# Quarter products of a pair issued in one piece, channel 128 moved ahead, 64-row transfers in a Fourier and MLP kernel

## The chip, the cores and the metric

One core of a Trainium2 chip runs the whole program. The metric is device time in microseconds (us), and lower is better. A measurement of this kernel can tell differences of about 0.2% (1.6 us).

## The reference

Float32 data, 2 batches of 3136 x 256 (sequence x channels), three blocks one after the other:

```python
# block 1: Fourier mixing along the sequence
X = np.fft.rfft(x, axis=1)
Yr, Yi = complex product of X with w_r + i w_i, plus bias
Y = soft threshold of Yr and Yi by 0.01
a = np.fft.irfft(Y, n=3136, axis=1)
# block 2: layer norm and MLP, 256 -> 1024 -> 256
m = a + relu(layernorm(a) * g_ln @ w_ch1) @ w_ch2
# block 3: 2-D Fourier transform, then a second MLP
u = m + real(np.fft.fft(np.fft.fft(m, axis=1), axis=2))
out = u + relu(layernorm(u) @ w1) @ w2
```

## The kernel before

3136 is 49 x 64, so each transform along the sequence is split into one of length 49 and one of length 64. Block 2 runs in 13 chunks (`mlp1`) and block 3 in 13 chunks (`mlp2`), mostly of 512 rows. A chunk has a first layer (`l1`, eight steps of six matmuls into a `psa` bank, L217 to L219; then relu on ScalarE, L744, and the rest term on VectorE, L746) and a second layer (`l2`, one step for each 128 rows: pairs of matmuls L763 and L764 into a `psb` bank, then VectorE adds L769 and L770). The input of a chunk is transposed through memory: VectorE transposes blocks (L684), `dT<-q` stores 512 KB (L690), `q<-dT` loads it back (L698), and then ScalarE and VectorE form the two operands of `l1` from `q`, as `u0r<-q` (L199 and L207).

The change concerns **stage 4**, the class `Stage98`: the transform of length 49 over block 2's output `dX` (one scratch tensor in DRAM of 98 x 8192 for each batch), giving `dA`. For each of eight column groups `g` a `step` does this:

- `load` (L380): two DMAs of 49 rows x 1024 columns into partitions 0 to 48 and 64 to 112 of a slot. One of four slots is used for each group; groups are loaded up to three ahead.
- `fold` (L392 to L394, GpSimd): sums and differences of mirrored channels, for batch 1 only. Batch 0 does the same after the product instead (`fold_last`, ScalarE L445 and VectorE L449 and L450).
- `quad` (L403): four quarter products of 49 x 64 by 49 x 512, over `e` (output half) and `s` (input half), into two `psc` banks. There are three `psc` banks.
- copies of both banks to `o` (ScalarE, L199), and two columns of channel 128, `o<-mid` (ScalarE for batch 0, GpSimd L453 for batch 1).
- four stores `dA<-o` of 49 x 512 (L455).

Channel 128 has no mirror partner. `middle` loads it for all groups (L412, `m<-dX`), and `middle2`, called from the step of `g == 0`, makes its product with a quad of 16 columns and copies it to `mid`.

Batch 0's stage 4 runs inside chunks 8 to 10 of `mlp1` and batch 1's inside chunks 1 to 3 of `mlp2`. Two tables say at which step (chunk, layer, step) each `g` is emitted; the later pieces of block 3 (`r<-dA`, L815; products L831 and L856 into `psc`; sums with `yb`, L861 to L868) read `dA`.

```python
STAGE4_AT = ((8, "l1", 7), (8, "l2", 1), (8, "l2", 3), (9, "l1", 1), (9, "l1", 6), (9, "l2", 2), (10, "l1", 3), (10, "l2", 0))
STAGE4_MLP2 = ((1, "l1", 3), (1, "l2", 0), (1, "l2", 2), (2, "l1", 1), (2, "l1", 5), (2, "l2", 1), (3, "l1", 1), (3, "l1", 5))
```

The order on each engine is set by a scheduler that simulates the program; `tc.issue_after(ins)` forces what is written under it to come behind `ins`, and `mark[...]` keeps the last instruction of a kind for that use. Each engine then runs its instructions strictly in that order. Nearly all DMAs are issued by SP, in one queue order, and each of them also waits for the DMA that stands eight places before it in that order, since eight completion semaphores are used in turn. The final rows of `mlp2` load `yb<-dX` (L635) and store `out_dram<-o` (L779), some of them with an outer size of 2 or with one row for each of 128 partitions.

Of the kernel before, what the change touches and what calls it, by code (L numbers as in the profile page):

```python
# [36 lines left out]
SOON = {"b": (3, 5), "mix": (5, 7), "stats": (("l1", 6), ("l2", 0)), "norm": (("l2", 0),) * 4, "flip": (("l2", 1), ("l2", 2))}  # L37
LATE = {"b": (4, 6), "mix": (6, 7), "stats": (("l1", 7), ("l2", 0)), "norm": (("l2", 0),) * 4, "flip": (("l2", 2), ("l2", 3))}
LAND_AT = ("l1", 3)
TRANS1_AT = (4, 6)  # L40
PREP0_AT = (23, 24, 26, 28)
L2_BEHIND = 7
APPLY_POOL = ()
STAGE4_AT = ((8, "l1", 7), (8, "l2", 1), (8, "l2", 3), (9, "l1", 1), (9, "l1", 6), (9, "l2", 2), (10, "l1", 3), (10, "l2", 0))
STAGE4_MLP2 = ((1, "l1", 3), (1, "l2", 0), (1, "l2", 2), (2, "l1", 1), (2, "l1", 5), (2, "l2", 1), (3, "l1", 1), (3, "l1", 5))
STAGE4_FROM = ((7, "l2", 0), (0, "l1", 5))
WARM_UP = 10
TB = 2
# [111 lines left out]
def fourier_moe_kernel(ctx, tc, x, w_r, w_i, b_r, b_i, g_ln, w11, w12, w21, w22,  # L160
# [59 lines left out]
        mark["pe"] = getattr(ins, "ins", ins)  # L220


    def scratch(nm):
        return [dp.tile([NQ, FW], F32, name=f"{nm}{b}") for b in range(NB)]

    dY, dX1, dA2 = (scratch(n) for n in ("dY", "dX1", "dA2"))

    def by_k1(t, k1, n):

# [1 line left out]
        return v[(k1 - 1) * 32768:(k1 - 1 + n) * 32768].rearrange("(k p c) -> p k c", k=n, c=D)  # L231

    def k1_zero(t):
        return t.rearrange("q f -> (q f)")[NK * 32768:].rearrange("(p c) -> p c", c=D)

    def rows(t, r0, n, nt):
        v = t.rearrange("q (j c) -> (q j) c", c=D)
# [24 lines left out]
    def behind(f):  # L262

        with ExitStack() as es:
            for k, ins in mark.items():
                if k not in ("pe", "clip", "hi"):
                    es.enter_context(tc.issue_after(ins))
            f()

# [94 lines left out]
    class Stage98:  # L364
# [1 line left out]


        def __init__(self, src, dst, tag):
            self.src, self.dst = (a.rearrange("(n s) f -> s n f", s=2) for a in (src, dst))
            self.tag, self.raw, self.out = tag, {}, {}  # L370
            self.fold_last = src is dX1[0]
            self.g = self.nl = self.ns = 0

        def load(self):
            g = self.nl
            if g >= 8:
                return
            t = next(s98_ring)
            for s in range(2):
                sp.dma_start(out=t[64 * s:64 * s + N1], in_=self.src[s][:, g * 1024:(g + 1) * 1024])  # L380
            self.raw[g] = [t[:, e * 512:(e + 1) * 512] for e in range(2)]
            self.nl += 1

# [14 lines left out]
        def quad(self, c, v, n=512):  # L398

            ps = [psum(self.tag) for _ in range(2)]  # L400
            for e in range(2):
                for s in range(2):
                    ins = nc.tensor.matmul(out=ps[s][64 * e:64 * e + 64, 0:n], lhsT=ca[64 * s:64 * s + N1, c:c + 64],  # L403
                                           rhs=v[e][64 * s:64 * s + N1], start=True, stop=True)
            mark["pe"] = getattr(ins, "ins", ins)
            return ps

        def middle(self):

            t = wk.tile([128, 32], F32, tag="m98", name="m98", bufs=1)  # L410
            for s in range(2):
                sp.dma_start(out=t[64 * s:64 * s + N1], in_=self.src[s].rearrange("n (j c) -> n j c", c=D)[:, :, 128])  # L412
            self.mid_in = t.rearrange("q (g e j) -> q e g j", e=2, j=2)

        def middle2(self):
# [14 lines left out]
        def step(self):  # L430
            g = self.g
            if g >= 8:
                return
            if g == 0:
                self.middle2()
            if self.nl <= g + 3:
                self.load()
            self.fold()
            ps = self.quad(0, self.raw.pop(g))
            for s in range(2):  # L440
                o = wk.tile([128, 512], F32, tag="r98", name="o98", bufs=R98) if self.fold_last and s else next(o98_ring)
                mid = self.mid[:, s, 2 * g:2 * g + 2]
                if self.fold_last:
                    v, w = (a.rearrange("q (j c) -> q j c", c=D) for a in (ps[s], o))
                    ins = nc.scalar.activation(out=w[:, :, 0:128], in_=v[:, :, 0:128], func=AF.Copy)  # L445
                    with tc.issue_after(getattr(ins, "ins", ins)):
                        a_copy(w[:, :, 128], mid)
                    lo, hi = w[:, :, 1:128], v[:, :, 255:128:-1]
                    nc.vector.tensor_tensor(out=w[:, :, 129:256], in0=lo, in1=hi, op=ALU.subtract)  # L449
                    nc.vector.tensor_tensor(out=lo, in0=lo, in1=hi, op=ALU.add)  # L450
                else:
                    a_copy(o, ps[s])
                    nc.gpsimd.tensor_copy(o[:, 128:512:256], mid)  # L453
                for e in range(2):
                    sp.dma_start(out=self.dst[s][:, (2 * g + e) * 512:(2 * g + e + 1) * 512], in_=o[64 * e:64 * e + N1])  # L455
            self.g += 1


# [156 lines left out]
    class Chunk:  # L615
# [112 lines left out]
        def l1(self, f):  # L728
            n = self.nt * 128
            (w1h, w1l), _ = self.wv  # L730
            ps = psum("a")
            fs = slice(f * 128, (f + 1) * 128)
            with ExitStack() as es:
                if self is mlp1[0] and f:
                    es.enter_context(tc.issue_after(self.pe))
                for c in range(2):
                    mm3r(ps[:, 0:n], w1h[:, c, fs], w1l[:, c, fs], self.xh[:, c, 0:n], self.xl[:, c, 0:n],
                         c == 0, c == 1)
            if f == L2_BEHIND:
# [12 lines left out]

        def l2(self, i):
            _, w2 = self.wv
            if not self.stored:
                self.o = oslot()
            self.stored += 1
            ps = psum("b")
            ts_ = slice(i * 128, (i + 1) * 128)
            with tc.issue_after(self.pe if self is mlp2[-1] and self.stored > 1 else self.last):  # L760
                for f in range(NF):
                    h, l = self.h[f]
                    nc.tensor.matmul(out=ps, lhsT=h[:, ts_], rhs=w2[:, f, :], start=f == 0, stop=False)  # L763
                    ins = nc.tensor.matmul(out=ps[:, 0:D], lhsT=l[:, ts_], rhs=w2[:, f, 0:D], start=False,  # L764
                                           stop=f == NF - 1)
            self.pe = getattr(ins, "ins", ins)

            o = self.o[:, i, :]
            nc.vector.tensor_tensor(out=o, in0=ps[:, 0:D], in1=self.y[:, i, :], op=ALU.add)  # L769
            nc.vector.tensor_tensor(out=o, in0=ps[:, D:2 * D], in1=o, op=ALU.add)  # L770
# [99 lines left out]
    def chunks2(plan, wv):  # L870
        cs = []
        for pairs in plan:
            lo, st, nt = [], [], 0
            for pr in pairs:
                for src, lst in ((dX1, lo), (out, st)):
                    for h, (b, k1) in enumerate(pr):
                        v = src[b] if src is out else src[b].rearrange("q (j c) -> (q j) c", c=D)
# [92 lines left out]
        todo.setdefault(k, []).append(f)  # L970
    for k, f in zip(MLP1_AT, mlp1_w[1:]):
        todo.setdefault(k, []).append(f)
    mlp1 = chunks1(0, wv1) + chunks1(1, wv1)
    mlp1[0].flipped = mlp1[1].flipped = False

# [217 lines left out]
    hook(2, "l2", 2, store3(4, range(4, 7)))  # L1193
    hook(*STAGE4_FROM[0], s4[0].start)
    hook(8, "l1", 1, after(8, 1, s4[0].ahead))
    for k, part, i in STAGE4_AT:
        hook(k, part, i, in_turn(mlp1, k, s4[0].step))
    mlp1[2].load()
# [47 lines left out]
```

## Time and profile before

| | us |
|---|---|
| median of 3 runs | 795.63 (795.11 to 795.73) |
| the profiled execution, whole time | 795.9 |
| its span, first to last instruction | 794.1 |
| TensorE (PE) busy | 782.5 (99%) |
| VectorE (DVE) busy | 550.6 (69%) |
| ScalarE (ACT) busy | 365.0 (46%) |
| GpSimd (POOL) busy | 127.5 (16%) |

The stretch of stage 4 is 354 to 420 us for batch 0 and 500 to 580 us for batch 1. A wait row names who waited, for whom, the us in total, the number of times and the longest. In a row of instructions, `[1.77 <-DVE mv L644]` is idle time before it and what ended it, and the us column is the length of one instruction, which for pipelined matmuls is longer than their spacing; the spacing is read from the start times. The granted clock of TensorE has two levels here, full and half; a window's figure is the mean (0.83 means that it was at half for a part).

### The profile page before, as it was taken

To read this page: it belongs to the slowest core of one execution; us is meant where nothing else is said; L and a number is where in the kernel's file an instruction comes from. 1 tells how busy PE (TensorE), PEld (TensorE's weight loads), DVE (VectorE), ACT (ScalarE), POOL (GpSimd) and SP (SyncE) were. 2 spreads that over 40 slices of the span, in tenths; PEclk is the share of its full clock that TensorE was granted. 3 is DMA by queue.
4 is the path that set the end of the run, shared out by engine and by line. 5 is a ranking of instruction groups with operands and counts; after the bars stand their busy time and mean duration, and the time that the engine had idled before them with its cause. 6 is when DMAs were issued, how large, how long until landed. Compare 5 with 4: busy or idle time off the path is not lost.

```text
span 794.1 us, 12190 instructions
## 1 busy us (share of the span) xinstructions
PE 782.5 (99%) x4348; PEld 652.9 (82%) x4348; DVE 550.6 (69%) x1253; ACT 365.0 (46%) x792; POOL 127.5 (16%) x146
## 2 busy tenths in 40 slices
PE   9999999999999999999999999998999999999997
PEld 3989977978888889976777988766788898888886
DVE  6799978687856988766666776456555757656643
ACT  0543356447954444645542344345443535444421
POOL 0465322254510111100000001243100000000000
PEclk9999999999999999999999999999999999999999
DMA  8950200621266323464543336534443334422211
GB/s 216 273 162 35 80 1 1 216 110 39 68 212 225 109 100 112 150 183 163 187 127 123 100 100 182 154 116 137 132 138 96 112 123 120 109 70 74 62 34 40
DMA packets 78047, 95.07 MB, mean 120 GB/s; under 512 B 17428, under 2 KB 59194, under 8 KB 77792
## 3 DMA queue, kind: packets, MB, share of 16 engines
q1 hardware_dynamic: 77908, 94.24, 38.3%
q8 instruction: 34, 0.56, 0.3%
q14 instruction: 25, 0.20, 0.1%
q10 hardware_dynamic: 80, 0.07, 0.0%
HBM read 56.80 MB, written 37.49 MB: 119 GB/s over the span
## 4 chain that ended last, share of the span: by engine, by line
PE 80%; DMA 9%; DVE 6%; issue 2%; SPq 1%; ACT 1%; POOL 1%; POOLq 0%; DVEq 0%; ACTq 0%
PE psb L763 21%; PE psa L217 11%; PE psb L764 11%; PE psa L219 10%; PE psa L218 10%; PE psb L511 5%; PE psc L831 2%; DMA q<-dT 2%; DMA dA<-o 2%; PE psc L356 2%; PE psa L478 2%; PE psc L403 2%; DMA q<-in_x_dram 1%; PE psc L856 1%; PE psc L532 1%
## 5 line engine op out<-in xcount | busy, mean ns | idle before, releaser
L744 ACT ACTIVATE h<-psa 128x512 fp32r<-128x512 f32 (+2 forms) x208 | 117.5, 572 | 209.2 <-PE psa L219 153.7
L746 DVE SCALAR_TENSOR_TENSOR h<-psa,h 128x512 fp32r<-128x512 f32 (+2 forms) x208 | 134.9, 653 | 63.5 <-ACT h L744 59.8
L763 PE MATMUL psb<-r2b,h 128*128 128x512 f32 x392 | 138.5, 400 | 1.8 <-DVE mv L644 1.8
L763 PE MATMUL psb<-r3a,h 128*128 128x512 f32 x392 | 137.3, 396 | 0.0
L764 PE MATMUL psb<-r2b,h 128*128 128x256 f32 x392 | 106.9, 282 | 0.0
L764 PE MATMUL psb<-r3a,h 128*128 128x256 f32 x392 | 106.1, 281 | 0.0
L511 PE MATMUL psb<-wm,h 128*128 128x256 f32 (+1 forms) x600 | 90.4, 296 | 0.2 <-DVE w L517 0.2
L763 PEld LDWEIGHTS psb<-r2b,h 128*128 128x128 f32 x392 | 72.5, 189 | 19.0 <-issue 3.8
L763 PEld LDWEIGHTS psb<-r3a,h 128*128 128x128 f32 x392 | 71.8, 188 | 16.3 <-ACT h L744 0.8
L511 PEld LDWEIGHTS psb<-wm,h 128*128 128x128 f32 (+1 forms) x600 | 78.1, 188 | 7.7 <-issue 5.6
L217 PE MATMUL psa<-u0r,r2b 128*128 128x512 f32 (+2 forms) x208 | 82.4, 396 | 2.0 <-ACT u0r L199 1.5
L217 PE MATMUL psa<-u0r,r3a 128*128 128x512 f32 (+1 forms) x208 | 80.0, 384 | 0.1
L219 PE MATMUL psa<-u0r,r2b 128*128 128x512 f32 (+2 forms) x208 | 79.5, 386 | 0.0
L218 PE MATMUL psa<-u0r,r2b 128*128 128x512 f32 (+2 forms) x208 | 79.2, 381 | 0.0
L218 PE MATMUL psa<-u0r,r3a 128*128 128x512 f32 (+1 forms) x208 | 78.8, 379 | 0.0
L764 PEld LDWEIGHTS psb<-r3a,h 128*128 128x128 f32 x392 | 73.9, 189 | 5.5 <-issue 1.6
L764 PEld LDWEIGHTS psb<-r2b,h 128*128 128x128 f32 x392 | 74.7, 190 | 2.9
L219 PE MATMUL psa<-u0r,r3a 128*128 128x512 f32 (+1 forms) x208 | 76.2, 378 | 0.0
L769 DVE TENSOR_TENSOR o<-psb,yb 128x256 f32<-128x256 f32 x74 | 30.3, 419 | 63.0 <-PE psb L764 62.6
L199 ACT ACTIVATE yg<-psc 98x512 f32<-98x512 f32 (+2 forms) x58 | 49.6, 867 | 37.9 <-PE psc L532 20.8
L217 PEld LDWEIGHTS psa<-u0r,r2b 128*128 128x128 f32 x208 | 39.6, 190 | 13.2 <-ACT u0r L199 2.8
L207 POOL TENSOR_TENSOR h<-w 128x512 f32<-128x512 f32 (+1 forms) x26 | 34.7, 1334 | 84.7 <-DVE w L518 78.1
(130 smaller groups left out, 1264.5 us busy)
## 6 DMA issues: line engine op xcount, KB each, us to landing
dT<-q SPq DMA_DIRECT2D x19, 512.0 KB
q<-dT SPq DMA_DIRECT2D x19, 512.0 KB
s<-in_moe_w_ch_dram SPq DMA_DIRECT2D x16, 512.0 KB
u0r<-dX SPq DMA_DIRECT2D x32, 196.0 KB
dA<-o SPq DMA_DIRECT2D x64, 98.0 KB
dY<-yg SPq DMA_DIRECT2D x12, 512.0 KB
r<-dA SPq DMA_DIRECT2D x48, 128.0 KB
dX<-o SPq DMA_DIRECT2D x10, 512.0 KB
```

What stands on the lines that cost most here:

```text
L199: nc.scalar.activation(out=o, in_=i, func=AF.Copy, scale=scale)
L207: ins = eng.tensor_tensor(out=o, in0=a, in1=b, op=ALU.subtract)
L217: nc.tensor.matmul(out=ps, lhsT=lh, rhs=rh, start=first, stop=False)
L218: nc.tensor.matmul(out=ps, lhsT=ll, rhs=rh, start=False, stop=False)
L219: ins = nc.tensor.matmul(out=ps, lhsT=lh, rhs=rl, start=False, stop=last)
L356: nc.tensor.matmul(out=ps[0:NQ, :], lhsT=tab["cim"], rhs=t, start=True, stop=True)
L511: nc.tensor.matmul(out=ps[0:m, u * D:(u + 1) * D], lhsT=xv[:, o:o + m], rhs=wm_hl[wv][:, e, c, :], start=k == 0, stop=k == 11)
L744: ins = nc.scalar.activation(out=h[:, 0:n], in_=ps[:, 0:n], func=AF.Relu)
L746: ins = nc.vector.scalar_tensor_tensor(out=l[:, 0:n], in0=ps[:, 0:n], scalar=0.0, in1=h[:, 0:n], op0=ALU.max, op1=ALU.subtract)
L763: nc.tensor.matmul(out=ps, lhsT=h[:, ts_], rhs=w2[:, f, :], start=f == 0, stop=False)
L764: ins = nc.tensor.matmul(out=ps[:, 0:D], lhsT=l[:, ts_], rhs=w2[:, f, 0:D], start=False, stop=f == NF - 1)
L769: nc.vector.tensor_tensor(out=o, in0=ps[:, 0:D], in1=self.y[:, i, :], op=ALU.add)
```

## The change

Six things are changed:

1. `quad` writes its four products in reverse order (`e` and `s` from 1 to 0), each forced behind the one before. It leaves `mark["quad"]`, and every `l1` and `l2` step written later is forced behind that mark.
2. `middle2` is no longer part of the step of `g == 0`. It has a hook of its own: (8, "l1", 6) in `mlp1`, (1, "l1", 2) in `mlp2`.
3. For batch 1, `o<-mid` is a ScalarE copy directly behind the copy of the bank, in place of a GpSimd copy.
4. Loads of stage 4 take 64 rows in place of 49, and stores write 64 rows. `dX` and `dA` get 128 rows in place of 98 so that this is in bounds.
5. `l_pad` fills rows 98 to 127 of each `dX` from the input `x` at the start of the program: two DMAs from DRAM to DRAM of 240 x 1024 (983 KB each), in SP's order between two loads of MLP weights.
6. The first table is moved: all of batch 0's groups but the first stand at other steps, with the last at (10, "l1", 2) in place of (10, "l2", 0). In the second table the first entry moves by one step.

```diff
-STAGE4_AT = ((8, "l1", 7), (8, "l2", 1), (8, "l2", 3), (9, "l1", 1), (9, "l1", 6), (9, "l2", 2), (10, "l1", 3), (10, "l2", 0))
-STAGE4_MLP2 = ((1, "l1", 3), (1, "l2", 0), ...
+STAGE4_AT = ((8, "l2", 0), (8, "l2", 2), (9, "l1", 1), (9, "l1", 4), (9, "l1", 7), (9, "l2", 1), (9, "l2", 3), (10, "l1", 2))
+STAGE4_MLP2 = ((1, "l1", 4), (1, "l2", 0), ...
...
-    dY, dX1, dA2 = (scratch(n) for n in ("dY", "dX1", "dA2"))
+    dY, dX1, dA2 = scratch("dY"), scratch("dX1", 128), scratch("dA2", 128)
...
-                sp.dma_start(out=t[64 * s:64 * s + N1], in_=self.src[s][:, g * 1024:(g + 1) * 1024])
+                sp.dma_start(out=t[64 * s:64 * s + 64], in_=self.src[s][:, g * 1024:(g + 1) * 1024])
...
-            for e in range(2):
-                for s in range(2):
-                    ins = nc.tensor.matmul(out=ps[s][64 * e:64 * e + 64, 0:n], lhsT=ca[64 * s:64 * s + N1, c:c + 64],
-                                           rhs=v[e][64 * s:64 * s + N1], start=True, stop=True)
-            mark["pe"] = getattr(ins, "ins", ins)
+            with ExitStack() as es:
+                for e in (1, 0):
+                    for s in (1, 0):
+                        ins = nc.tensor.matmul(out=ps[s][64 * e:64 * e + 64, 0:n], lhsT=ca[64 * s:64 * s + N1, c:c + 64],
+                                               rhs=v[e][64 * s:64 * s + N1], start=True, stop=True)
+                        mark["pe"] = getattr(ins, "ins", ins)
+                        es.enter_context(tc.issue_after(mark["pe"]))
+            mark["quad"] = mark["pe"]
...
-            if g == 0:
-                self.middle2()
...
-                    nc.gpsimd.tensor_copy(o[:, 128:512:256], mid)
+                    a_copy(o[:, 128:512:256], mid)
...
-                    sp.dma_start(out=self.dst[s][:, (2 * g + e) * 512:(2 * g + e + 1) * 512], in_=o[64 * e:64 * e + N1])
+                    sp.dma_start(out=self.dst[s, g, e], in_=o[64 * e:64 * e + 64])
...
+                if "quad" in mark:
+                    es.enter_context(tc.issue_after(mark["quad"]))
...
+    def l_pad(b):
+        sp.dma_start(out=dX1[b][NQ:128].rearrange("q (k f) -> q k f", k=8), in_=x[b].rearrange("k q f -> q k f")[0:128 - NQ])
...
+    hook(8, "l1", 6, in_turn(mlp1, 8, s4[0].middle2))
+    hook(1, "l1", 2, in_turn(mlp2, 1, s4[1].middle2))
```

On TensorE, in chunk 9 of `mlp1`, this is the fourth quad of batch 0 among the matmuls of `l1` before (`psc<-u0r,ca` are the quarter products, x2 is half of a quad):

```order
L219 MATMUL psa<-u0r,r3a 128x512
L403 MATMUL psc<-u0r,ca 64x512 x2
L217 MATMUL psa<-u0r,r3a 128x512
L218 MATMUL psa<-u0r,r3a 128x512
L219 MATMUL psa<-u0r,r3a 128x512
L217 MATMUL psa<-u0r,r3a 128x512
L218 MATMUL psa<-u0r,r3a 128x512
L219 MATMUL psa<-u0r,r3a 128x512
L403 MATMUL psc<-u0r,ca 64x512 x2
L217 MATMUL psa<-u0r,r3a 128x512
```

and now, at the same quad:

```order
L218 MATMUL psa<-u0r,r3a 128x512
L219 MATMUL psa<-u0r,r3a 128x512
L220 MATMUL psa<-u0r,r3a 128x512
L406 MATMUL psc<-u0r,ca 64x512 x4
L218 MATMUL psa<-u0r,r3a 128x512
L219 MATMUL psa<-u0r,r3a 128x512
L220 MATMUL psa<-u0r,r3a 128x512
```

The two halves have become one piece. The first quad of batch 0 stood in two halves as well (together with the small product of channel 128) and is in one piece now; the other fourteen were in one piece before too.

On SP, in chunks 1 and 2 of `mlp2`, the DMAs from the last `u0r` loads of stage 4 to the transposed input of the chunk after next (`dT<-q`) stood like this before (`dA<-o` are stage 4's stores, `yb` and `out_dram` belong to the chunks):

```order
L380 DMA u0r<-dX_69 49x1024
L455 DMA dA_71<-o_1756 49x512 x4
L380 DMA u0r<-dX_69 49x1024
L635 DMA yb<-dX_68 64x256 x2
L779 DMA out_dram<-o 64x256 x2
L635 DMA yb<-dX_68 128x1x256
L779 DMA out_dram<-o 2x64x256
L380 DMA u0r<-dX_69 49x1024
L455 DMA dA_71<-o_1756 49x512 x4
L380 DMA u0r<-dX_69 49x1024 x3
L690 DMA dT_194<-q 128x2x512
```

and stand like this now:

```order
L458 DMA dA_71<-o_1758 64x512 x4
L382 DMA u0r<-dX_69 64x1024 x4
L638 DMA yb<-dX_68 64x256
L787 DMA out_dram<-o 64x256 x2
L458 DMA dA_71<-o_1758 64x512 x4
L787 DMA out_dram<-o 2x64x256
L638 DMA yb<-dX_68 64x256
L693 DMA dT_194<-q 128x2x512
L638 DMA yb<-dX_68 128x1x256
```

Four `u0r` loads are now asked for together, ahead of the stores of the second quad, and the three that stood directly ahead of `dT<-q` are gone from there.

On ScalarE, in chunk 1 of `mlp2` at the first quad of batch 1, the order was this (`mid<-psc` copies the product of channel 128, `u0r<-q` is the operand of the next chunk):

```order
L199 ACTIVATE w<-psc 128x256
L199 ACTIVATE mid<-psc 128x16
L744 ACTIVATE h<-psa 128x512 x3
L199 ACTIVATE mid<-psc 128x16
L199 ACTIVATE o_1756<-psc 128x512 x2
L744 ACTIVATE h<-psa 128x512
L199 ACTIVATE u0r<-q 128x512 x2
```

and is now:

```order
L200 ACTIVATE o_1758<-psc 128x512
L200 ACTIVATE o_1758<-mid 128x2
L200 ACTIVATE o_1758<-psc 128x512
L200 ACTIVATE o_1758<-mid 128x2
L749 ACTIVATE h<-psa 128x512 x2
L869 ACTIVATE w<-psc,w 128x65
L869 ACTIVATE w<-psc,w 128x64
L749 ACTIVATE h<-psa 128x512
L200 ACTIVATE u0r<-q 128x512 x2
```

The two copies of channel 128 stand among the copies of the banks now, and three relus and one correction step (`w<-psc,w`) lie between the quad's copies and `u0r<-q`, where one relu lay before.

## Rows read from the trace of the kernel before

**Rows 1.** Page, busy time by engine: us, share of span, instructions.

```profile
PE 782.5 (99%) x4348; PEld 652.9 (82%) x4348; DVE 550.6 (69%) x1253; ACT 365.0 (46%) x792; POOL 127.5 (16%) x146
```

**Rows 2.** Waits of PE, 345 to 435 us (first row) and 495 to 600 us.

```profile
PE psc L831 <- DMA r<-dA: 0.4, 1, 0.4
...
PE psb L763 <- DVE mv L644: 1.8, 1, 1.8
PE psa L217 <- ACT u0r L199: 1.5, 1, 1.5
PE psa L217 <- DVE h L746: 0.5, 1, 0.5
```

**Rows 3.** Windows: length; busy PE, PEld, DVE, ACT, POOL; granted clock, DMA share, GB/s.

```profile
520.00:530.00 10.00, 8.66 (x42) 6.50 (x43) 6.16 (x18) 6.11 (x15) 6.64 (x16) 0.83 0.27 73
...
550.00:560.00 10.00, 8.52 (x39) 6.09 (x32) 5.18 (x13) 6.17 (x15) 1.88 (x5) 0.83 0.31 95
```

**Rows 4.** Timeline of PE behind its longest wait: start, length, instruction.

```profile
521.34 0.47 PE L763 MATMUL psb<-r2b,h 128*128 128x512 f32 x1 [1.77 <-DVE mv L644]
...
522.48 0.63 PE L763 MATMUL psb<-r2b,h 128*128 128x512 f32 x1
...
525.04 0.63 PE L763 MATMUL psb<-r2b,h 128*128 128x512 f32 x1
```

**Rows 5.** Chain of work that ended last, 500 to 560 us: start, length, what.

```profile
496.80 8.96 DMA dT<-q
...
506.49 9.28 DMA q<-dT
515.79 0.64 ACT u0r L199
...
527.99 8.19 DMA dA<-o
...
542.53 9.10 DMA q<-dT
551.65 0.64 ACT u0r L199
...
553.07 0.71 PE psa L219
...
556.74 0.23 PE psa L218
```

**Rows 6.** Timeline of SP's queue: start, time spent issuing, DMAs.

```profile
483.25 9.62 SPq L380 DMA_DIRECT2D u0r<-dX  x10
...
528.39 4.65 SPq L380 DMA_DIRECT2D u0r<-dX  x3
534.35 0.39 SPq L690 DMA_DIRECT2D dT<-q  x1
```

**Rows 7.** Windows as in rows 3, chosen for what the DMA engines move.

```profile
60.00:72.00 12.00, 12.00 (x83) 11.15 (x82) 10.74 (x17) 4.76 (x10) 7.21 (x7) 1.00 0.00 1
...
488.00:492.00 4.00, 4.00 (x22) 3.36 (x20) 2.84 (x7) 3.14 (x8) 2.83 (x5) 1.00 0.46 183
...
643.00:645.00 2.00, 2.00 (x18) 2.00 (x17) 1.45 (x5) 1.18 (x5) 0.00 (x0) 1.00 0.14 50
671.50:673.00 1.50, 1.50 (x10) 1.31 (x9) 1.50 (x5) 0.60 (x1) 0.00 (x0) 1.00 0.80 216
```

**Rows 8.** Timeline of PE around quads of batch 0: start, length, instruction.

```profile
355.82 0.30 PE L403 MATMUL psc<-m,ca 49*64 49x16 f32 x8
...
371.19 0.28 PE L764 MATMUL psb<-r3a,h 128*128 128x256 f32 x1
...
371.54 0.28 PE L764 MATMUL psb<-r3a,h 128*128 128x256 f32 x1
371.75 1.09 PE L403 MATMUL psc<-u0r,ca 49*64 49x512 f32 x8
...
373.10 0.39 PE L219 MATMUL psa<-u0r,r3a 128*128 128x512 f32 x1
...
374.49 0.39 PE L219 MATMUL psa<-u0r,r3a 128*128 128x512 f32 x1
374.81 1.08 PE L403 MATMUL psc<-u0r,ca 49*64 49x512 f32 x4
...
376.15 0.39 PE L218 MATMUL psa<-u0r,r3a 128*128 128x512 f32 x1
```

**Rows 9.** Groups by line, 340 to 430 us (ACT) and 500 to 580 us (POOL): busy, mean ns, idle before.

```profile
L199 ACT ACTIVATE o<-mid 128x2 f32<-128x2 f32 x16 | 3.2, 201 | 0.0
...
L453 POOL COPY o<-mid 128x2 f32<-128x2 f32 x16 | 2.8, 188 | 24.0 <-ACT o L199 24.0
```

More of the change, by code (lines that the diff above doesn't have):

```diff
@@ L39 @@
 LAND_AT = ("l1", 3)
+PAD_AT = (15, 17)
 TRANS1_AT = (4, 6)
@@ L43 @@
 APPLY_POOL = ()
-STAGE4_AT = ((8, "l1", 7), (8, "l2", 1), (8, "l2", 3), (9, "l1", 1), (9, "l1", 6), (9, "l2", 2), (10, "l1", 3), (10, "l2", 0))
-STAGE4_MLP2 = ((1, "l1", 3), (1, "l2", 0), (1, "l2", 2), (2, "l1", 1), (2, "l1", 5), (2, "l2", 1), (3, "l1", 1), (3, "l1", 5))
+STAGE4_AT = ((8, "l2", 0), (8, "l2", 2), (9, "l1", 1), (9, "l1", 4), (9, "l1", 7), (9, "l2", 1), (9, "l2", 3), (10, "l1", 2))
+STAGE4_MLP2 = ((1, "l1", 4), (1, "l2", 0), (1, "l2", 2), (2, "l1", 1), (2, "l1", 5), (2, "l2", 1), (3, "l1", 1), (3, "l1", 5))
 STAGE4_FROM = ((7, "l2", 0), (0, "l1", 5))
@@ L220, in mm3r, with scratch @@
         mark["pe"] = getattr(ins, "ins", ins)
-    def scratch(nm):
-        return [dp.tile([NQ, FW], F32, name=f"{nm}{b}") for b in range(NB)]
-    dY, dX1, dA2 = (scratch(n) for n in ("dY", "dX1", "dA2"))
+    def scratch(nm, n=NQ):
+        return [dp.tile([n, FW], F32, name=f"{nm}{b}") for b in range(NB)]
+    dY, dX1, dA2 = scratch("dY"), scratch("dX1", 128), scratch("dA2", 128)
     def by_k1(t, k1, n):
@@ L233, in k1_zero @@
     def k1_zero(t):
-        return t.rearrange("q f -> (q f)")[NK * 32768:].rearrange("(p c) -> p c", c=D)
+        return t.rearrange("q f -> (q f)")[NK * 32768:NK * 32768 + N2 * D].rearrange("(p c) -> p c", c=D)
     def rows(t, r0, n, nt):
@@ L265, in behind @@
             for k, ins in mark.items():
-                if k not in ("pe", "clip", "hi"):
+                if k not in ("pe", "clip", "hi", "quad"):
                     es.enter_context(tc.issue_after(ins))
@@ L368, in __init__ @@
         def __init__(self, src, dst, tag):
-            self.src, self.dst = (a.rearrange("(n s) f -> s n f", s=2) for a in (src, dst))
+            self.src = src.rearrange("(n s) f -> s n f", s=2)
+            self.dst = dst.rearrange("(r s) (g e c) -> s g e r c", s=2, e=2, c=512)
             self.tag, self.raw, self.out = tag, {}, {}
@@ L411, in middle @@
             for s in range(2):
-                sp.dma_start(out=t[64 * s:64 * s + N1], in_=self.src[s].rearrange("n (j c) -> n j c", c=D)[:, :, 128])
+                sp.dma_start(out=t[64 * s:64 * s + 64], in_=self.src[s].rearrange("n (j c) -> n j c", c=D)[:, :, 128])
             self.mid_in = t.rearrange("q (g e j) -> q e g j", e=2, j=2)
@@ L759, in l2 @@
             ts_ = slice(i * 128, (i + 1) * 128)
-            with tc.issue_after(self.pe if self is mlp2[-1] and self.stored > 1 else self.last):
+            with ExitStack() as es:
+                es.enter_context(tc.issue_after(self.pe if self is mlp2[-1] and self.stored > 1 else self.last))
+                if "quad" in mark:
+                    es.enter_context(tc.issue_after(mark["quad"]))
                 for f in range(NF):
@@ L876, in chunks2 @@
                     for h, (b, k1) in enumerate(pr):
-                        v = src[b] if src is out else src[b].rearrange("q (j c) -> (q j) c", c=D)
+                        v = src[b] if src is out else src[b].rearrange("q (j c) -> (q j) c", c=D)[0:N]
                         lst.append((slice(h * 64, h * 64 + 64), nt, 1,
@@ L972, in fourier_moe_kernel @@
         todo.setdefault(k, []).append(f)
+    def l_pad(b):
+        sp.dma_start(out=dX1[b][NQ:128].rearrange("q (k f) -> q k f", k=8), in_=x[b].rearrange("k q f -> q k f")[0:128 - NQ])
+    for b in range(NB):
+        todo.setdefault(PAD_AT[b], []).append(lambda b=b: l_pad(b))
     mlp1 = chunks1(0, wv1) + chunks1(1, wv1)
```

## Prediction

> **What bounds the kernel now.** The first view is the busy time by engine: TensorE (PE) is busy for 782.5 of 794.1 us [rows 1], so 11.6 us at most can come from idle time, and anything else must come from TensorE's own work or its clock. The second is the table of waits of PE in the stretches that the change touches. Around batch 0's stage 4 there is one wait of 0.4 us; around batch 1's there are three, 1.8, 1.5 and 0.5 us [rows 2], together 4.2 us. The third is the table of windows: the two that hold the long waits show a granted clock of 0.83 over 10 us [rows 3], while the windows without such a wait stand at 1.00. So a long wait is paid twice. Behind the 1.77 us wait four pairs of L763 and L764 take from 522.48 to 525.04, 0.64 us each [rows 4]; the clock is at its lower level there.
>
> The fourth view, the chain of work, says where the waits come from. The first is held by ScalarE and VectorE, which start on the chunk's operand at 515.79, when `q<-dT` has landed; that load took 9.28 us and the store before it, `dT<-q`, 8.96 us. The second is the same with a `q<-dT` of 9.10 us that lands at 551.65. The wait of 0.5 us goes back to a `dA<-o` store that took 8.19 us [rows 5]. None of these is arithmetic: stage 4's transfers and the chunks' transfers share one SP queue and the DMA engines. SP needs 9.62 us to issue ten `u0r` loads and 4.65 us for three more directly ahead of a `dT<-q` [rows 6].
>
> **Part by part.** *64 rows.* While only 49-row transfers are in flight, the share of busy DMA engines is 0.46 and 183 GB/s are moved. A transfer with an outer size of 128 reaches 0.80 and 216 GB/s, one with an outer size of 2 or one row for each partition 0.14 and 50 GB/s [rows 7]. 0.46 is near 7 of 16 engines and 49 is 7 x 7. In the Trainium skill, "DMA: Bandwidth & Descriptors", section "Why a DMA increments its semaphore by 16 and not by 1", the number of engines is the largest up to 16 that divides the slowest dimension of both sides; this trace agrees (0.46 and 0.14 for 7 and 2 of 16). The ten loads move 10 x 49 x 4 KB = 2.0 MB in some 10.9 us at 183 GB/s; at 64 rows they are 2.62 MB. The ends are 216 GB/s (12.1 us, a loss of 1.2 us; its packets are small) and 183/0.46 = 398 GB/s (6.6 us, a gain of 4.3 us). I take the second, since its packets are those of these loads. The 64 `dA<-o` stores should gain in the same ratio.
>
> *First wait.* What stands behind the ten loads on SP is `dT<-q` and then the `q<-dT` that lands at 515.79 [rows 5, 6]. It must land 1.77 us earlier for the wait to go. Of 4.3 us, 2.5 are left over. So 1.8 us of wait go, and with them the slow clock: five pairs of 0.64 us against 0.35 (371.19 to 371.54, [rows 8]) is 5 x 0.29 = 1.5 us. What is late next is the same operand's path through VectorE, which the order of its correction steps sets. I allow for that below.
>
> *Second wait.* The three `u0r` loads that hold SP for 4.65 us directly ahead of `dT<-q` (534.35) are gone from there: four now stand together, ahead of the stores of the second quad, and two behind the `q<-dT`. 4.65 us is more than the 1.5 us of the wait. Its clock loss: eight matmuls from 553.07 to 556.74 take 3.67 us, at 0.23 us [rows 5] they would take 1.84, so 1.8 us. Both go: 3.3 us. The moved `u0r` loads wait for folds on GpSimd, and while they stand at SP's head, the stores and `dT<-q` behind them stand too; this is the slower rival below.
>
> *Two short waits.* The 0.5 us behind a `dA<-o` of 8.19 us and the 0.4 us of `r<-dA` behind such stores [rows 2, 5] go with faster stores: 0.9 us.
>
> *Quads in one piece.* A whole quad (x8) pushes the next matmul from 371.54 + 0.12 (L764 has a third of a pair's 0.35) to 373.10 - 0.23, that is 1.2 us; a half (x4) from 374.49 + 0.23 to 376.15 - 0.23, the same 1.2 us [rows 8]. A half costs as much as a whole, since the four quarters run side by side. Two of sixteen quads stood in halves, both in batch 0, where PE waits for nothing else: 2 x 1.2 = 2.4 us go. Reversing the order within a quad changes nothing in this sum; the bounds are 0 and the 1.2 us of one more half if a quarter no longer ran beside its partner, and I take 0.
>
> *Channel 128 in a place of its own.* Its row is 0.30 us long [rows 8] and it stood against a half quad, where the work around it was switched once for both. Standing alone it costs between 0 and the 0.2 us by which a quad's 1.2 us exceed its own 1.0 us, for each batch. I take 0.3 us for both. The Trainium skill, "TensorEngine Tiling (Array Packing)", section "Key Properties", says that a change of tiling mode drains the engine; it speaks against this edit, and by it alone I would take both ends in full, 0.4 us. No row here shows the drain apart from the products.
>
> *`o<-mid` on ScalarE.* Sixteen copies of 0.2 us replace sixteen of 0.19 us on GpSimd, each of which came behind ScalarE's copy anyway [rows 9]. 3.2 us more on ScalarE, which is 46% busy [rows 1]; the stores no longer cross to another engine. Where a relu stands right behind them, it comes 0.4 us later, in a chain that PE has a bank to spare for. I take 0; the end is 8 x 0.4 = 3.2 us if every quad's relu were waited for.
>
> *Pads.* Two transfers of 0.98 MB between weight loads. From 60 to 72 us nothing is moved [rows 7]; at 216 GB/s they need 9.1 us, which fits, so 0. At the 50 GB/s of the slowest form they would take 39 us and hold back a weight load by some 27 us, but the MLP that needs it starts long after. That would cost 0 to 3 us through VectorE's decoding.
>
> *New small waits.* Batch 0's quads come closer together (the last a chunk part earlier), and each brings four operations on VectorE. Batch 1's first quad needs two of three `psc` banks among the correction steps. I allow 0.6 us, about the one short wait of this kind in rows 2, with ends 0 and 3.
>
> **The sum.** -1.8 - 1.5 - 1.5 - 1.8 - 0.9 - 2.4 + 0.3 + 0.6 = -9.0 us. The profiled execution took 795.9 us, 1.8 more than its span, and 0.3 more than the median of 795.63. 795.9 - 9.0 = 786.9 in its frame, and 786.6 for the median.
>
> **The rivals.** (A) *One of the two long waits stays.* For it: the two slow transfers, `out_dram` of 2 rows and `yb` of one row for each partition at 50 GB/s [rows 7], still stand directly ahead of each `q<-dT`, so their time stays and the load may land no more than a microsecond or two earlier. Against it: the loads ahead of them move up as a block. One wait with its clock is 3.3 us: 789.9. (By the page of the Trainium skill named above, these two forms are left at 2 engines by this change; that is a reason for A, and its price stays the same.) (B) *Both stay:* the 64-row transfers move 31% more bytes and win nothing beyond that, so the queue is as late as before. Left are the quads and half a microsecond: 795.6 - 2.4 + 0.3 - 0.5 = 793.0. (C) *No change:* the wait is hidden by what comes next: the quads' 2.4 us are made up by new waits of 0.5 us at some of the sixteen quads, since those are now pinned in the row while `psc` banks come free late; with the transfers as in B that is 795.6, within 0.2%. (D) *Slower:* SP's queue is blocked by four `u0r` loads that wait for GpSimd's folds. The stores behind them land late, the copies to `o` wait, the relus behind these on ScalarE too, and PE stops with a clock loss of 3.3 us each time. From the fourth such stop it decides (three are 9.9 against 9.6 gained before the allowance); five of the eight quads of batch 1 stand behind such loads, which is 795.6 - 9.6 + 5 x 3.3 = 802.5. Against it: the longest wait of this kind in the trace is 0.5 us, and there are few.
>
> **How the numbers follow.** Forecast 0.48, A 0.20, B 0.13, C 0.10, D 0.09. The predicted time is that of the forecast, 786.6. The forecast's own ends are 784.0 (no new wait, and stores that free a little more) and 789. For 8 in 10 the range goes on over A to B, 793.5, and leaves out C, D. About 0.2% is what a measurement of this kernel can tell from no change. Forecast, A and B are faster by more than that: 0.81; C is 0.10; D 0.09.
>
> **What would show it.** Right: in the timeline of PE no split quad; in the waits of PE between 495 and 600 us no line over 0.6 us; granted clock 1.00 in all windows there; a DMA share near 1 while stage 4's loads run, and SP's time for ten loads well under 9.6 us. PE's busy time falls by about 5.5 us (quads 2.4, clock 3.3). Wrong: a clock under 1 anywhere past 350 us, PE waiting for `u0r` or for `psc`, or ten loads that take SP as long as before. If the time falls by only 2 to 3 us while `q<-dT` still takes 9 us, then B holds, and the quads were the only gain.

## The result, and the profile after

| | median us | runs | ratio to before, 95% interval |
|---|---|---|---|
| before | 795.68 | 4 | 1 |
| changed kernel | 785.99 | 4 (785.52 to 788.16) | 0.9882 (0.9861 to 0.9904) |
| changed kernel, another chip | 787.31 (before there: 796.66) | 6 | 0.9892 (0.987 to 0.9914) |

The profiled execution took 785.59 us against 795.9, with a span of 783.8 us. The page of the changed kernel and its waits of PE from 340 to 620 us, where [rows 1] and [rows 2] stood before:

```profile
PE 775.1 (99%) x4348; PEld 650.5 (83%) x4348; DVE 552.4 (70%) x1253; ACT 368.8 (47%) x808; POOL 125.9 (16%) x130
```

```profile
PE psb L771 <- DVE sm L655: 1.4, 1, 1.4
```

One wait of four is left. It is the first of the two long ones: the rows of the windows (columns as in [rows 3]) show PE busy for 8.55 of 10 us there. The matmul that ended the second wait at 552.33 us starts at 544.05 us now, without a wait, and nothing is lost from 550 to 560 us either. The clock is 1.00 in these two windows, and in all others from 500 to 600 us:

```profile
510.00:520.00 10.00, 8.55 (x48) 6.34 (x48) 6.09 (x16) 7.39 (x20) 5.36 (x9) 1.00 0.85 205
550.00:560.00 10.00, 10.00 (x59) 7.79 (x58) 4.93 (x13) 4.17 (x10) 1.55 (x3) 1.00 0.43 128
```

Where did the 10.3 us come from? TensorE does the same number of `psb` matmuls in both kernels, so the same one, counted from the start of the program, can be compared. Number 1273, behind all of batch 0's stage 4, and number 1681, behind batch 1's, begin here (timeline of PE, before and then after):

```profile
438.32 0.39 PE L763 MATMUL psb<-r3a,h 128*128 128x512 f32 x1
...
612.60 0.39 PE L763 MATMUL psb<-r2b,h 128*128 128x512 f32 x1
```

```profile
434.61 0.39 PE L771 MATMUL psb<-r3a,h 128*128 128x512 f32 x1
...
602.19 0.39 PE L771 MATMUL psb<-r2b,h 128*128 128x512 f32 x1
```

So 3.7 us are won by the end of batch 0's stage 4, 6.7 us more in batch 1's, and next to nothing outside. These are two single executions: up to 0.9 us of the 3.7 need not come from the change. In `b_loads_behind` below, every engine has in batch 0 the same order as in the kernel before, and there number 1273 begins at 437.39 instead of 438.32, without the 0.4 us wait for `r<-dA`. The queue of SP looks like this now (where [rows 6] stood):

```profile
479.13 10.00 SPq L382 DMA_DIRECT2D u0r<-dX  x10
...
502.71 0.56 SPq L701 DMA_DIRECT2D q<-dT  x1
...
519.34 0.53 SPq L693 DMA_DIRECT2D dT<-q  x1
529.69 0.75 SPq L701 DMA_DIRECT2D q<-dT  x1
```

The ten loads take SP 10.00 us, not less than the 9.62 before. The store `dT<-q` that stood at 534.35 is issued at 519.34: 15.0 us earlier, although TensorE's work around it is only 6 to 7 us earlier. VectorE's transposes, which make what it stores, stood like this before and stand like this now (timeline of VectorE):

```profile
526.37 1.31 DVE L684 STREAM_TRANSPOSE q<-q 128x512 f32<-128x512 f32 x2
```

```profile
517.73 1.30 DVE L687 STREAM_TRANSPOSE q<-q 128x512 f32<-128x512 f32 x2 [2.10 <-ACT q L674]
```

The store came 6.7 us behind their end before (527.7), and 0.3 us behind it now. That is the first sign that order won here, and not the speed of the transfers.

### The profile page after: what moved, and what is told of

It is laid out like the page before. It is cut to its first block, busy times and chain, and to the rows that moved or that the text cites. A ratio compares the mean times of both kernels' runs of the same rounds, so it can differ in the third digit from the quotient of the medians.

```text
span 783.8 us, 12173 instructions
## 1 busy us (share of the span) xinstructions
PE 775.1 (99%) x4348; PEld 650.5 (83%) x4348; DVE 552.4 (70%) x1253; ACT 368.8 (47%) x808; POOL 125.9 (16%) x130
## 4 chain that ended last, share of the span: by engine, by line
PE 88%; DVE 4%; DMA 4%; issue 1%; SPq 1%; ACT 1%; POOL 0%; DVEq 0%; POOLq 0%
PE psb L771 23%; PE psa L218 12%; PE psb L772 12%; PE psa L220 11%; PE psa L219 11%; PE psb L514 5%; PE psc L839 3%; PE psc L406 2%; PE psc L357 2%; PE psa L481 2%; DMA q<-in_x_dram 1%; PE psc L864 1%; PE psc L535 1%; DMA q<-dT 1%; DMA stg<-dY 1%
## 5 line engine op out<-in xcount | busy, mean ns | idle before, releaser
L771 PE MATMUL psb<-r2b,h 128*128 128x512 f32 x392 | 136.8, 396 | 1.4 <-DVE sm L655 1.4
```

## The experiments

Theory 1 is the prediction's: transfers of 64 rows use more DMA engines and relieve the queue, and with that the waits go. Theory 2 grew from the rows above: the order does it (where the quads stand, and what stands ahead of what on SP), and the 64 rows bring nothing. Each kernel is compared with the kernel before on its own chip, and the ratio carries over to the 795.6 us of the expectations. The changed kernel itself was run again on only one of the three chips of the experiments (`a_again`).

**Parts alone and parts undone: the 64 rows.** `b_rows64` is the kernel before with the new `load`, stores, scratch and padding; TensorE's order stays the same. `a_rows49` is the changed kernel with the old ones:

```diff
-                sp.dma_start(out=t[64 * s:64 * s + 64], in_=self.src[s][:, g * 1024:(g + 1) * 1024])
+                sp.dma_start(out=t[64 * s:64 * s + N1], in_=self.src[s][:, g * 1024:(g + 1) * 1024])
...
-                    sp.dma_start(out=self.dst[s, g, e], in_=o[64 * e:64 * e + 64])
+                    sp.dma_start(out=self.dst[s][:, (2 * g + e) * 512:(2 * g + e + 1) * 512], in_=o[64 * e:64 * e + N1])
```

> The kernel before with only the 64-row transfers, the padded scratch and its two filling DMAs; TensorE's order is unchanged, on SP two of the three u0r loads ahead of the dT<-q at 534 us move behind it. Theory 1 (the queue is relieved by transfers on more DMA engines): both long waits shrink or go, their clock loss and the short waits with them, 5 to 7 us, so 789 to 791 us. Theory 2 (the ten loads take SP 10.0 us after as against 9.62 before, so the rows bring nothing; the order of the work does it): 794.5 to 796.5 us, with waits of 1.5 us and more and a clock under 1 between 515 and 560 us.

> The changed kernel with 49-row transfers and without the padding; TensorE's order is unchanged. Theory 1: the waits of PE between 495 and 600 us and the slow clock come back, 4 to 7 us, so 790 to 793 us. Theory 2: within 1 us of the changed kernel, 785 to 787 us.

`b_rows64` measured 794.31 us, 0.9968 (0.9954 to 0.9982): 2.5 us or 793.1 on the scale of 795.6, not 5 to 7 us, but more than theory 2 allowed too. `a_rows49` measured 787.09 us, 0.9869 (0.9853 to 0.9885): the whole gain is there without the 64 rows. Theory 1 falls. Two rows of windows show why; they lie in the ten `u0r` loads, of the changed kernel first and of `a_rows49` second:

```profile
484.00:489.00 5.00, 5.00 (x31) 4.32 (x29) 3.54 (x8) 3.41 (x9) 3.06 (x6) 1.00 1.01 240
```

```profile
484.00:489.00 5.00, 5.00 (x28) 4.22 (x26) 3.49 (x11) 4.14 (x11) 2.38 (x5) 1.00 0.46 187
```

With 64 rows all DMA engines are busy (1.01 against 0.46), and yet the rate rises only from 187 to 240 GB/s, 1.28 times, for 64/49 = 1.31 times the bytes. A load takes as long as before; more engines are each slower (240/1.01 = 238 GB/s for a full share, against 187/0.46 = 407). What holds them back no run shows. In its profile `b_rows64` is ahead by 0.9 us at matmul 1273, without the wait for `r<-dA` in [rows 2]; but `b_loads_behind`, which has the same order there and 49 rows, is ahead by as much, so the rows did not do that. The rest is the clock, which stayed at 1.00 behind waits of 1.8 and 1.4 us that were both still there.

**The quads alone.** `b_quad` is the kernel before with the new `quad` and the lines that force `l1` and `l2` behind it:

```diff
+            with ExitStack() as es:
+                for e in (1, 0):
+                    for s in (1, 0):
...
+                if "quad" in mark:
+                    es.enter_context(tc.issue_after(mark["quad"]))
```

> The kernel before with only the quads held together and the l1 and l2 steps forced behind them; transfers, tables and channel 128 as before. Theory 1: the two split quads are worth 2.4 us and no wait goes, so 793 us. Theory 2: the order matters for the waits as well, so below 791 us if they go, and 793 us only if it is the other edits' order that counts.

796.02 us, 0.9984 (0.9973 to 0.9996), 794.3 on the scale of 795.6: a gain of 1.3 us, less than either theory expected, since new waits took more than the 2.4 us. Timeline of PE at batch 0's first quad (a quarter product is two records, so x8 is a whole quad):

```profile
356.63 0.30 PE L404 MATMUL psc<-m,ca 49*64 49x16 f32 x8
356.76 1.05 PE L404 MATMUL psc<-u0r,ca 49*64 49x512 f32 x2
360.08 1.08 PE L404 MATMUL psc<-u0r,ca 49*64 49x512 f32 x6 [2.27 <-ACT mid L199]
```

Channel 128's product and the quad want four `psc` banks, and there are three. The first quarter runs, the others wait until ScalarE has copied `mid`, and ScalarE has two operations ahead of that which themselves waited 1.3 us for a `q<-dT`. Before, the quad's second half could wait while `l2` went on; pinned, it stops all of TensorE. From 360 to 370 us the granted clock was 0.83 in that run. But the second long wait, the one of 0.5 us and the one for `r<-dA` are gone in `b_quad` as well, with 49 rows and the old tables: `dT<-q`, issued 6.7 us behind the end of VectorE's transposes in the kernel before, goes 2.0 us behind it there (timelines of VectorE and SP):

```profile
526.73 1.30 DVE L687 STREAM_TRANSPOSE q<-q 128x512 f32<-128x512 f32 x2 [1.67 <-ACT q L674]
```

```profile
529.98 1.17 SPq L693 DMA_DIRECT2D dT<-q  x1
```

Of the waits of before only the first stayed, at 2.9 us.

**Channel 128 back in the first step.** The changed kernel with `middle2` where it was:

```diff
+            if g == 0:
+                self.middle2()
...
-    hook(8, "l1", 6, in_turn(mlp1, 8, s4[0].middle2))
-    hook(1, "l1", 2, in_turn(mlp2, 1, s4[1].middle2))
```

> The changed kernel with channel 128's product back in the step of g = 0, directly ahead of the first quad. If that product and a held quad together need four psc banks of three (the run with the quads alone waited 2.3 us there, and its clock fell between 340 and 440 us), each batch pays such a wait: 2 to 4 us for one with its clock, so 788 to 793 us on the scale of 795.6 for the kernel before. If its place does not matter: within 0.5 us of the changed kernel, 786 us.

791.02 us, 0.9912 (0.989 to 0.9933), some 2.4 us slower than the changed kernel by the ratios, which is at the edge of what their intervals can tell. The same wait is there, in batch 0 alone, not in both as expected (timeline of PE):

```profile
358.48 1.05 PE L406 MATMUL psc<-u0r,ca 49*64 49x512 f32 x2
361.49 1.08 PE L406 MATMUL psc<-u0r,ca 49*64 49x512 f32 x6 [1.96 <-ACT mid L200]
```

So edit 2 is what lets edit 1 keep its gain in batch 0.

**Held but not spaced.** The quarters of a quad are still forced each behind the one before (held), but `l1` and `l2` are no longer forced behind the quad (spaced), so that their matmuls may come in between:

```diff
-                if "quad" in mark:
-                    es.enter_context(tc.issue_after(mark["quad"]))
```

> The changed kernel without l1 and l2 being forced behind the quad. In its order one quarter stands apart from the other three in six quads of batch 0 and one of batch 1. If a piece costs 0.7 to 1.2 us whatever its size (a half and a whole quad cost 1.2 us each): 7 more pieces, 5 to 8 us slower than the changed kernel, 791 to 794 us, nearly all of it in batch 0. If a single quarter hides beside other matmuls: 786 to 788 us.

799.32 us, 1.0021 (1.0007 to 1.0036), 797.3 on the scale of 795.6: slower than expected, and the only form of the changed kernel that lost the whole gain. In the trace one quarter stands apart in five quads of batch 0, not six, and in one of batch 1. Timeline of PE at one of the five:

```profile
372.83 0.28 PE L767 MATMUL psb<-r3a,h 128*128 128x256 f32 x1
373.04 1.07 PE L406 MATMUL psc<-u0r,ca 49*64 49x512 f32 x2
374.04 0.50 PE L220 MATMUL psa<-u0r,r3a 128*128 128x512 f32 x1
374.38 0.40 PE L218 MATMUL psa<-u0r,r3a 128*128 128x512 f32 x1
...
375.30 0.39 PE L219 MATMUL psa<-u0r,r3a 128*128 128x512 f32 x1
375.61 1.08 PE L406 MATMUL psc<-u0r,ca 49*64 49x512 f32 x6
376.62 0.50 PE L220 MATMUL psa<-u0r,r3a 128*128 128x512 f32 x1
376.96 0.39 PE L218 MATMUL psa<-u0r,r3a 128*128 128x512 f32 x1
```

One quarter (x2) is as long as three (x6), 1.07 and 1.08 us, and pushes the next matmul by as much: 372.83 + 0.12 to 374.38 - 0.23, and 375.30 + 0.23 to 376.96 - 0.23, 1.2 us both times. Over the same 270 `psb` matmuls, which span batch 0's quads, the changed kernel took 108.1 us and this one 114.3: 6.1 us for five more pieces, 1.2 us each. The rest was lost in batch 1, where a quad waited 4.6 us for `psc` and the mean clock was 0.66 from 550 to 560 us:

```profile
PE psc L406 <- ACT o L200: 4.6, 1, 4.6
```

```profile
550.00:560.00 10.00, 6.76 (x22) 4.23 (x23) 6.71 (x20) 7.27 (x20) 3.05 (x6) 0.66 0.34 79
```

**The old tables**, with all the rest of the change:

```diff
+STAGE4_AT = ((8, "l1", 7), (8, "l2", 1), (8, "l2", 3), (9, "l1", 1), (9, "l1", 6), (9, "l2", 2), (10, "l1", 3), (10, "l2", 0))
+STAGE4_MLP2 = ((1, "l1", 3), (1, "l2", 0), ...
```

> The changed kernel with the two tables of before. If the tables set where the waits of mlp2 lie: waits over 1.4 us and a slow clock come back, 788 to 792 us. If the pinning of l1 and l2 behind the quads does: within 1 us of the changed kernel, 785 to 787 us.

791.23 us, 0.9917 (0.9891 to 0.9942), some 2.8 us slower by the ratios, whose intervals still overlap. In its profile PE waited 0.9 us for a `psb` bank at 391 us, in batch 0, and 2.3 us at the first wait of batch 1, with a clock of 0.86 there. The second long wait did not come back. The tables are worth 0.35% by these ratios, some 30% of the gain; from one kernel on another chip that is an estimate.

**Channel 128's copies on GpSimd again:**

```diff
-                    a_copy(o[:, 128:512:256], mid)
+                    nc.gpsimd.tensor_copy(o[:, 128:512:256], mid)
```

> The changed kernel with the copy of channel 128 back on GpSimd for batch 1; TensorE's order is unchanged. Both theories: 786 us within 0.5 us if the copies lie beside other work; up to 1.5 us slower if GpSimd, which was fully busy while VectorE made the late operand at 512 us, holds the stores back.

787.91 us, 0.9882 (0.9861 to 0.9903): the same as the changed kernel. Edit 3 brings nothing that can be measured.

**Only SP's order, in the kernel before.** The loads of the last two groups of batch 1 behind `dT<-q`, with 49 rows, split quads and all other engines as they were:

```diff
+                if g >= 6 and not self.fold_last:
+                    es.enter_context(tc.issue_after(mlp2[3].trip))
```

> The kernel before with one thing changed: the u0r loads of the last two groups of batch 1 are forced behind the dT<-q that they stood ahead of on SP. The order on TensorE, VectorE and ScalarE is unchanged and all transfers have 49 rows. If SP's order makes the second long wait (1.5 us and its clock): dT<-q is issued some 5 us earlier and that wait goes, 1.5 to 3.3 us, 792.3 to 794 us on the scale of 795.6. If the transfers' speed does: no change, 795 to 796 us.

796.08 us, 0.9992 (0.9977 to 1.0008): no gain. Yet the mechanism did what it should, as far as it reached (timeline of SP; then of PE, with its waits from there on):

```profile
528.08 0.39 SPq L693 DMA_DIRECT2D dT<-q  x1
...
537.66 3.05 SPq L383 DMA_DIRECT2D u0r<-dX  x2
540.75 0.41 SPq L701 DMA_DIRECT2D q<-dT  x1
```

```profile
550.34 0.50 PE L217 MATMUL psa<-u0r,r2b 128*128 128x512 f32 x1 [0.29 <-ACT u0r L199]
551.23 0.50 PE L219 MATMUL psa<-u0r,r2b 128*128 128x512 f32 x1 [0.15 <-DVE u0r L207]
552.36 0.50 PE L219 MATMUL psa<-u0r,r2b 128*128 128x512 f32 x1 [0.17 <-DVE u0r L207]
...
606.55 0.58 PE L217 MATMUL psa<-u0r,r2b 128*128 128x512 f32 x1 [1.98 <-ACT u0r L199]
```

`dT<-q` went 6.3 us earlier, but two of the moved loads now stood ahead of `q<-dT` for 3.05 us, so that went only 1.8 us earlier. The wait at 550 us shrank from 1.5 to 0.6 us and the clock stayed up behind it. Then the gain was given back: at 606 us the operand of a later chunk came late, 1.98 us, and the clock fell there (0.84 from 600 to 610 us). In the changed kernel `q<-dT` for that chunk stands at 583.27 us instead of 599.05, and there is no wait.

**The same with VectorE's two adds first**, that is, the adds that empty the held `psb` bank ahead of the late operand (L207) in chunk 1:

```diff
+                    if ch is mlp2[1]:
+                        es.enter_context(tc.issue_after(ch.added))
```

> The same, and VectorE's two adds of the held psb bank ahead of the late operand in chunk 1 of mlp2. The quads stay split and the transfers stay at 49 rows. If the two orders make the two long waits: both shrink to under 0.8 us, 3.3 to 6.6 us, 789 to 792.3 us. If not: 793 to 796 us.

795.33 us, 0.9986 (0.9973 to 0.9998). The first wait was 2.3 us instead of 1.8, now for those adds themselves, so in the kernel before the operand ahead of them was not all that they waited for; at 550 us 1.2 us were left, and the wait at 606 us was 2.2 us. Two local orders do not replace the change.

**The adds first, in the changed kernel**, with 64 and with 49 rows (the same lines), and the changed kernel once more:

> The changed kernel with VectorE's two adds of the tile that holds the psb bank ahead of the operand of the late q<-dT, in chunk 1 of mlp2; TensorE's order is unchanged. If the wait of 1.4 us that is left there comes from VectorE's order (it sat idle for 3.2 us before the operand while the tile was done): the wait goes, 1.5 to 3 us faster than the changed kernel, 783 to 784.5 us. If the operand's lateness only moves the wait to the next l1: no gain, 785.5 to 786.5 us.

> The changed kernel with the two adds first and with 49-row transfers and no padding. If the 64 rows bring nothing: 0.984 as with 64 rows, 1.5 to 3 us faster than the changed kernel. If they help once the wait is gone: 785.5 to 787 us, no better than the changed kernel.

> The changed kernel again, on the chip of the other three, to compare with them: 786 us on the scale of 795.6, a ratio of 0.986 to 0.990.

With 64 rows: 784.94 us, 0.9843 (0.9824 to 0.9861), the fastest kernel of all. The wait that was 1.4 us (2.3 us in the profile of `a_again`) is 0.65 us (timeline of PE):

```profile
513.06 0.47 PE L771 MATMUL psb<-r2b,h 128*128 128x512 f32 x1 [0.65 <-DVE o L778]
```

Against 0.9882 and 0.9892 of the changed kernel that is 0.4% to 0.5%, about 3 to 4 us, from different chips. With 49 rows: 0.9878 (0.9858 to 0.9898), on the chip where the changed kernel had 0.9892, and with waits of 1.7 and 0.8 us left in its profile. So the adds first help, and with them the 64 rows may be worth 2 to 3 us; those two were not on one chip, and this stays open.

**All waits side by side.** Idle time of PE over 0.25 us from 300 us on, in the profile of each run (where, and how long, in us):

| run | batch 0 | first | second | others in batch 1 |
|---|---|---|---|---|
| before | 0.43 | 1.77 | 1.48 | 0.51 |
| `b_rows64` | | 0.53, 1.78 | 1.40 | 0.65, 0.73 |
| `b_loads_behind` | | 0.69, 1.81 | 0.29 | 1.98 |
| `b_both_orders` | 0.37 | 2.32 | 0.85 | 0.28, 2.16 |
| `b_quad` | 2.27, 0.94 | 2.94 | | 0.32 |
| `a_not_spaced` | | | 4.60, for `psc` | |
| `a_mid_first_step` | 1.96 | 0.78 | | |
| `a_old_tables` | 0.94 | 2.28 | | |
| `a_poolmid` | | 2.27 | | |
| `a_rows49` | | 2.13 | | |
| changed kernel, twice | | 1.45; 2.28 | | |
| `a_adds_first` | | 0.65 | | |
| `a_adds_first_49` | | 1.67 | | 0.76 |

Every kernel in which the quads are held and spaced is free of the second wait, with either size of transfer and either table; every kernel without has it or pays elsewhere. With held and spaced quads, the empty places in batch 0 need the new place of channel 128 and the new table on top. Each row is one execution: the first wait of the changed kernel itself differs by 0.8 us between two, and the 0.4 us of batch 0 come and go without any change there (`before` against `b_loads_behind`).

## Why the prediction was right, point by point

The time, 786.6 forecast and 785.99 measured, and the sign were right. The sum was -9.0 us and the profiled execution moved by -10.3. But how close it came is partly luck. Edit 4, which by the working was to end the first wait and the two short ones (with the clock, 4.2 of the 9.0 us), brought nothing that the changed kernel needs (`a_rows49`), and other effects filled its place. The signs that the prediction named were divided as well. No quad is split, the clock is 1.00 and the share is near 1, as it should be. But one wait over 0.6 us is left, and ten loads take SP as long as before, which was named as a sign of being wrong. PE's busy time fell by 7.4 us, not 5.5, and its idle time by 2.9 (11.6 to 8.7), where the sum had 3.6. The terms one by one:

- **Quads in one piece, -2.4 us: right.** A piece costs the same whatever it holds, and `a_not_spaced` shows it from the other side (1.2 us for each piece with one quarter). But the term left out its condition: held quads need `psc` banks at once. The rival C named that place; in `b_quad` it happened.
- **Channel 128 in a place of its own, +0.3 us: right in sum**, wrong in what it is for: it keeps the quad from a wait of 2 us. In batch 0 of the changed kernel the `l1` matmul behind the product would follow at 353.96 + 0.23 = 354.19 without it and follows in effect at 354.85 - 0.23 = 354.62. That is 0.43 us, against 0.12 beside a half quad before. The 0.3 us all lie in batch 0, more than the end of 0.2 us that was set for one batch; in batch 1 half of the product had stood alone before too (at 502.04 us), so nothing was added there. Timeline of PE:

```profile
353.96 0.39 PE L220 MATMUL psa<-u0r,r3a 128*128 128x512 f32 x1
354.28 0.30 PE L406 MATMUL psc<-m,ca 49*64 49x16 f32 x8
...
354.85 0.39 PE L219 MATMUL psa<-u0r,r3a 128*128 128x512 f32 x1
```

- **64 rows, the wrong step.** I took 398 GB/s from 183 GB/s and a share of 0.46, as if each engine kept its rate. Measured: 240 GB/s at a share of 1.01. The other end, 216 GB/s, was the near one, but only by chance: its window takes in the slow start of one `q<-dT` load. From 672.5 us on that load moves 349 GB/s at a share of 1.15 (last section), so that row did not speak for the form of these loads either. The 4.3 us for the ten loads did not come; SP spent 10.00 us on them.
- **First wait, -1.8 us: wrong, since it hung on that step.** It is 1.45 us in this profile and 2.3 us in the other. **Its clock loss, -1.5 us: right**, though not for the reason given; the wait stayed and the clock did not fall. This is luck in part: with the same order on TensorE the clock did fall behind such a wait in the profile of `a_poolmid`.
- **Second wait and its clock, -3.3 us: right.** The reason (SP's order: the loads ahead of `dT<-q`) holds for the wait itself, as `b_loads_behind` shows, but not for the end: without the rest a later wait takes it back. What ends it is edit 1, as the table shows; that it does so through the order that it brings about on SP fits `b_quad` (2.0 us in place of 6.7) but is not shown apart.
- **Short waits, -0.9 us: right in size.** They also go with 49 rows (`b_quad`, `a_rows49`), so faster stores were not what freed them. The 0.4 us for `r<-dA` need no change at all to go (`b_loads_behind`), so only the 0.5 us can be put down to the order.
- **`o<-mid` on ScalarE and the pads, 0: right**, as far as `a_poolmid` and `a_rows49` (without pads) can tell.
- **New small waits, +0.6 us: none.**
- **Not in the sum:** a matmul spacing of 0.48 instead of 0.23 us at 409.7 us in batch 0 (0.4 us with the next one), the products right behind the wait for `r<-dA`, which ran slowly (0.5 us, of which 0.2 us were gone in `b_loads_behind` too), and the products of L831 between `psb` matmuls 1273 and 1681, from start to the start of what follows, 11.3 us before (without the 0.5 us wait behind one of them) and 11.1 after. With the 0.6 us above these are 1.7 us. The first wait gave 1.5 us less than the sum had, and the whole moved 1.3 us further than the sum, so about 1 us stays unassigned.

Rival A (one long wait stays) came half true: it stayed, without its clock loss. Rival B's premise, that 64 rows win nothing beyond their bytes, was true of the loads; its time was not, because the order won what the rows did not. Rival D did not occur, but a stop of its size did in the unspaced kernel, for a different cause (copies to `o` late for `psc`).

What is not settled is how much of the 6.7 us of batch 1 is the earlier `dT<-q` (519.34 against 534.35) and `q<-dT` in itself. That SP's order changed with the pins is shown, and that moving loads alone is not enough; an order of SP like that of the changed kernel, with split quads, was not tried. Nor were edits 1 and 2 alone: `a_rows49` has the new tables and `a_old_tables` the 64 rows besides.

## What to carry to other kernels

A set of products that share the array belongs together in the order and has to be fenced from both sides: held alone, it split in more places than before (six quads against two). Pin such a block only when all banks that it fills are free by then, and move small neighbours that take one of them. A transfer on more engines is worth its extra bytes only where a row shows the higher rate for that very form, over a window that it fills; a higher busy share is not a higher rate.

## What the runs showed of the hardware

**More engines, no more speed for these loads.** Share 1.01 and 240 GB/s for 64-row loads, 0.46 and 187 for 49-row ones. The full share is not the limit in itself: in the kernel before, one `q<-dT` load moves 349 GB/s here (columns as in [rows 3]):

```profile
672.50:673.00 0.50, 0.50 (x5) 0.45 (x4) 0.50 (x2) 0.00 (x0) 0.00 (x0) 1.00 1.15 349
```

The Trainium skill, "DMA: Bandwidth & Descriptors", section "Why a DMA increments its semaphore by 16 and not by 1", gives the number of engines, and the shares agree with it; no run here shows a gain in time that would follow from that number.

**A wait does not always cost clock.** Waits of 1.48 and 1.77 us in the kernel before were followed by the lower of the two levels, while waits of 1.45 us (changed kernel), 1.8 us (`b_rows64`), 2.1 us (`a_rows49`) and 2.3 us (`a_again`) were not. Two kernels with the same order on TensorE and the same wait of 2.3 us differ: PE's busy time and clock in `a_again` and then in `a_poolmid`:

```profile
510.00:520.00 10.00, 7.72 (x49) 5.10 (x41) 4.32 (x13) 5.89 (x16) 3.51 (x6) 1.00 0.89 228
```

```profile
510.00:520.00 10.00, 7.73 (x36) 5.88 (x38) 5.47 (x15) 5.70 (x14) 3.41 (x8) 0.83 0.88 221
```

It also differs between executions of one kernel. Of `b_loads_behind`, three with a mean clock of 1.000 took 793.4 to 794.9 us and five at 0.996 took 795.0 to 799.3 us. The six of `a_again` have mean clocks of 0.997 to 1.000, with 790.94 us at 0.997 and 786.5 us at 0.999 and 1.000, though another at 0.997 took 787.65 us. So a clock term belongs into the range of a prediction rather than into its sum.

**VectorE beside GpSimd.** The two subtractions for the late operand took 1.84 us in the changed kernel, where GpSimd was busy with folds all the time, and 1.29 us before and in the kernel with the adds first, where it was idle beside them. In all fourteen traces every slow one of these operations, 0.8 to 1.2 us in place of 0.7, lies beside a busy GpSimd, but not every one beside a busy GpSimd is slow. Timeline of VectorE, and a window with GpSimd busy for 1.00 of 1.00 us:

```profile
511.40 1.84 DVE L208 TENSOR_TENSOR u0r<-q,u0r 128x512 fp32r<-128x512 f32 x2 [3.21 <-ACT u0r L200]
```

```profile
512.00:513.00 1.00, 0.87 (x6) 0.51 (x4) 1.00 (x2) 0.37 (x1) 1.00 (x2) 1.00 1.02 318
```

That is 0.55 us of the wait of 1.45 that was left, since the adds that PE waited for follow on VectorE. It is not what makes the wait: in `a_poolmid` these operations took 1.29 us, and the wait was 2.27 us.
